# Attention heads and weight preparation in a new order: slots of broadcasts, weight loads, clearing and conversion steps

## The chip, the cores and the metric

The kernel runs on one core of a Trainium2 chip. The metric is device time in microseconds (us); a number without a unit is us. Five engines work side by side, each through its own queue in order: TensorE (PE; PEld is its weight load), VectorE (DVE), ScalarE (ACT), GpSimd (POOL) and SyncE (SP), which here only issues DMA transfers. ScalarE issues a few transfers too.

## What is computed

Attention with rotary embedding over 4 batches of 8 heads, 576 positions of 64 numbers, and then a feed-forward layer with softplus over the 2304 tokens of 512 numbers:

```python
q_rot, k_rot = (rotate(q), rotate(k))
scores = scale * np.matmul(q_rot, k_rot.transpose(0, 1, 3, 2))
attn = np.exp(scores - np.max(scores, axis=-1, keepdims=True))
attn = attn / (np.sum(attn, axis=-1, keepdims=True) + 1e-09)
x = np.matmul(attn, v)          # then heads side by side: (2304, 512)
h = x @ w_in                    # (512, 2048)
g = np.maximum(h, 0.0) + np.log1p(np.exp(-np.abs(h)))
return g @ w_out                # (2048, 512)
```

The weights come as 64-bit floats (the kernel sees int64 words); everything else is float32. A float32 operand of a matmul is split into a rounded part and a rest (names ending in h and l, or two planes of one tile), and products of the parts are summed.

## The kernel before, in words

**Slots.** Attention is written as one loop over slots `s`, five slots to a head (`h, c = divmod(s, 5)`; `c` is the slot's place in the head, and so is the last digit of `s` modulo 5). 32 heads make 160 slots. In one slot three pipelined stages work on different heads: `p1(s)` computes a block of scores of 128 rows and `tensor_reduce` its row maxima on VectorE; nine slots later (`LAG`, `n2 = s - 9`) `p2(n2)` computes the transposed scores with the maxima already subtracted, `exps` takes two exponentials on ScalarE and `low` the rest on VectorE; three slots after that (`n3 = s - 12`) `pv_mm` multiplies with V. `pv_mm` of a head's last block is followed by `evac`, a copy of the sum from PSUM by ScalarE, in slot 1 of a head.

**Shift rows.** The maxima of a head enter `p2` as two extra rows (64 and 65 of plane 1) of its tile `qs`. They take this way: GpSimd splits them (`shift1`, slot 0), TensorE transposes them and ScalarE copies them to `shr` (`shift2`, slot 1), and a transfer that ScalarE issues puts them into `qs` (`shift3`, L487, after the exponentials of slot 1). The first `p2` of that head (slot 4) needs them. There are four `qs` tiles (`NST`), so once `p2` is through with a head, the two rows are cleared for the `p1` of the head four later: L636 and L637, a ScalarE copy from a tile `zero`, which GpSimd zeroes at the start (L594).

**SyncE's order.** `chain` puts the transfers that SyncE issues one behind the other as the program writes them: for each pair of heads two raw tiles of q and k (590 KB each), per head the stacking of q and k from the rotated tiles (`stack_q`, `stack_k`), V, the store of the result (`store`), and in given slots

- a half of a weight chunk: `load_p(f, n)` in the slots of `LOADS`, 262 KB each, f the block of weights, n the half (two halves make a chunk, four a block); each chunk takes a buffer, for f = 1 of the two `wr`, else of the three `wraw`, which turn round;
- a broadcast of reciprocals of row sums: `load_r` (L186), 147 KB, 16 in all, the eight heads of batch 0 and then of batch 1, from slot `XL` on, every fifth slot. The reciprocals of a batch are made by `recip` (L569 an addition, L570 the reciprocal, both on VectorE), in slots 62, 102 and 142 for batches 0, 1 and 2.

**Conversions.** For the first three blocks the weights are converted during attention: `PLAN` has a tuple of nine slots for each of the six chunks. `conv_w` is resumed in each: a ScalarE step (L138) in the first slot and one (L151) in the second, four pieces of bit operations on VectorE (L142, L146) in the third to sixth, which are the last to read the raw tile, an addition on GpSimd (L162), a ScalarE copy (L165) in the eighth and a subtraction on GpSimd (L167). So per chunk three ScalarE steps, in the first, second and eighth slot of its tuple.

**Afterwards.** From slot 146 (`XS`) on GpSimd multiplies and splits the attention results (`split_xb`); after slot 169 the feed-forward stage begins (`emit_h`, `emit_o`), which prepares the rest of the weights beside its matmuls.

`pin` keeps an instruction in program order on its engine. GpSimd rotates q and k (`rope_steps`, one step a slot, L325 and L322), VectorE places the first pair at the start (`place_pair0`).

Of the kernel before, what the change touches and what calls it, by code (L numbers as in the profile page):

```python
# [19 lines left out]
S = 576  # L20
# [3 lines left out]
NB = 4  # L24
NH = 8
# [5 lines left out]
FC = 3  # L31
SEG = 4
XS = 146
XL = 73
WP = 160
LAG = 9
PVD = 3
NST = 4
# [3 lines left out]
PB = 5  # L42
CW = 512
AHEAD = 2
PLAN = ((78, 80, 81, 84, 86, 89, 90, 93, 95), (88, 90, 91, 94, 96, 99, 100, 103, 105),
        (98, 100, 104, 106, 109, 111, 115, 118, 120), (108, 110, 114, 116, 119, 121, 125, 128, 130),
        (120, 123, 124, 126, 129, 131, 135, 138, 140), (130, 133, 134, 136, 139, 144, 145, 148, 150))
LOADS = {43: (0, 0), 48: (0, 1), 53: (0, 2), 58: (0, 3), 63: (1, 0), 68: (1, 1), 73: (1, 2), 78: (1, 3), 83: (2, 0),
         88: (2, 1), 93: (2, 2), 98: (2, 3), 103: (3, 0), 108: (3, 1), 138: (3, 2), 143: (3, 3), 148: (4, 0), 153: (4, 1)}
SPLITS = {146: 2, 148: 0, 153: 0}  # L50
LEAD = 3
ROPES = {1: ((1, 2),), 2: ((1, 4),), 3: ((1, 1),), 5: ((1, 2),), 9: ((2, 1),), 10: ((2, 1),), 11: ((2, 1),),
# [7 lines left out]
def rope_attention_softplus_moe(  # L60
# [8 lines left out]
    nc = tc.nc  # L69
# [19 lines left out]
    pin = tc.keep_in_program_order  # L89
# [191 lines left out]
    def attention(es, es_r, es_s, tail):  # L281
# [11 lines left out]
        zero = at1.tile([128, S], F32, name="zero")  # L293
# [23 lines left out]
        def rnd(out, in_, e):  # L317
            if e == "A":
                pin(nc.scalar.copy(out=out, in_=in_))
            else:  # L320
                e = nc.vector if e == "V" else nc.gpsimd
                pin(e.tensor_scalar(out=out, in0=in_, scalar1=1.0, scalar2=0.0, op0=ALU.mult, op1=ALU.add))  # L322
# [268 lines left out]
            nc.gpsimd.memset(ks[i][64:128, 1, :].bitcast(F32), 0.0)  # L591
            nc.gpsimd.memset(ks[i][64:66, 1, :].bitcast(F32), 1.0)
        nc.gpsimd.memset(sh0.bitcast(F32), 0.0)
        nc.gpsimd.memset(zero[64:66], 0.0)  # L594
        for i in range(2):
            nc.gpsimd.memset(vs[i][:, :, 1, :].bitcast(F32), 1.0)
        place = place_pair0()
# [6 lines left out]
        for s in range(NSLOT + LAG + PVD):  # L604
            n2, n3 = s - LAG, s - LAG - PVD
            h, c = divmod(s, 5)
            r = s + 4
            if r % 10 == 0 or s == 0:
                p = r // 10 + 1
                for _ in rope:  # L610
                    pass
                rope = rope_steps(p) if 2 < p < NP else iter(())
            has2, has3 = 0 <= n2 < NSLOT, 0 <= n3 < NSLOT
            if has3 and (c != 0 or s > NSLOT):
                pv_mm(n3)
                if n3 % 5 == 4:
                    evac(n3 // 5)
                has3 = False
            if n2 < NSLOT:
                tile2(n2)  # L620
            if has2:
                p2(n2)
            shr = shift2(h - 1, n2) if s > 6 and c == 1 and s <= NSLOT + 1 else None
            if has2:
                exps(n2)
            if shr is not None:
                shift3(h - 1, shr)
            if has3:
                pv_mm(n3)
            if s < NSLOT:  # L630
                p1(s)
                if s == LAG - 2:
                    shift_first()
            if has2:
                low(n2)
            if n2 > 0 and n2 % 5 == 0 and n2 // 5 - 1 + NST < NB * NH:  # L636
                rnd(qs[(n2 // 5 - 1) % NST][64:66, 1, :S], zero[64:66], "A")  # L637
            if s >= 5 and c == 0 and s <= NSLOT:
                shift1(h - 1)
            if s == 15:  # L640
                next(sv)
            if s < NSLOT:
                if s < 2:
                    next(place)
                for p, z in ROPES.get(s, ()):
                    for _ in range(z):
                        next(pairs[p], None)
                if s == 2:
                    next(place)
                for g, i, j, a in STACKS.get(s, ()):  # L650
                    if i:
                        stack_k(g, chain, (j,))
                    else:
                        stack_q(g, chain, j, a)
                if s != 16:
                    next(rope, None)
                if s in (20, 22):
                    next(rope, None)
                g = (s + 6) // 5
                if s % 10 == 4 and 14 < s and g < NB * NH:  # L660
                    stack_q(g, chain)
                    stack_k(g, chain, (0,))
                if s % 10 == 5:
                    for _ in rope:
                        pass
                    if 15 < s and g < NB * NH:
                        stack_k(g, chain, (1,))
                if s % 10 in (2, 7) and 2 < s // 10 + 2 < NP:
                    load_pair(s // 10 + 2, (s % 10 // 7,))
                if s % 10 == 9 and s > 10 and g < NB * NH:  # L670
                    stack_q(g, chain)
                    stack_k(g, chain)
                if c == 0:
                    load_v(h)
            if c == 2 and 0 < h <= NB * NH:
                sv = split_v(h - 1)
                next(sv)
            if c == 4 and s != 14:
                next(sv, None)
            if done and c == 2:  # L680
                store(*done.pop(), chain)
            if n3 % (5 * NH) == 5 and n3 > 5:
                load_sums(n3 // (5 * NH) - 1, chain)
            if n3 % (5 * NH) == 10 and n3 > 10:
                recip(n3 // (5 * NH) - 1)
            tail(s)
        return recip

# [20 lines left out]
    with ExitStack() as es:  # L709
# [5 lines left out]
        def tail(s):  # L715
            if s == NSLOT - 9:
                es_r.close()
            i, j = divmod(s - XL, 5)
            if 0 <= i < 2 * NH and j == 0:
                load_r(*divmod(i, NH))  # L720
            if s in LOADS:
                load_p(*LOADS[s])
            for n, slots in enumerate(PLAN):
                if s == slots[0]:
                    k = divmod(n, 2)
                    early[n] = conv_w([k], CW, pin, 1, {0: pre.pop(k)}, nc.gpsimd, True)
                    next(early[n])
                if s in slots:
                    next(early[n], None)
            if s in (WP, WP + 5):  # L730
                next(late[s > WP])
            if s >= XS:
                for _ in range(2 if s > NSLOT else SPLITS.get(s, 1 if s % 5 else 0)):
                    next(splits, None)
            if s == NSLOT + LAG - 1:
                es_s.close()
                mp["h"] = pool(ctx, "ps_h", 2, space=PSUM)
                mp["t"] = pool(ctx, "t", 1)
                mp["g"] = pool(ctx, "g", NG)
            if NSLOT + LAG <= s < NSLOT + LAG + AHEAD:  # L740
                ahead.append(units[len(ahead)])
                emit_h(*ahead[-1])
            if s >= NSLOT + LAG and w.dtype != F32:
                convert()
# [92 lines left out]
```

## Time and profile before

| | us |
|---|---|
| median of 3 runs | 733.25 |
| the runs | 731.91 to 736.65 |
| the profiled execution | 732.48 |
| its span, first to last instruction | 730.60 |
| TensorE busy (share of the span) | 715.8 (98%) |
| VectorE | 493.6 (68%) |
| ScalarE | 413.7 (57%) |
| GpSimd | 318.6 (44%) |

A row of the profile has the start and the length of an instruction or of some of one kind (x4: four of them), what it writes and reads (out<-in), and in brackets the idle time of its engine before it with what ended that. L637 is line 637. Where a helper issues many operations, they all have its line: L319 is ScalarE's, L325 and L322 are VectorE's and GpSimd's. A "q" behind an engine's name (SPq, ACTq) is its queue of issues.

### The profile page before, as it was taken

Reading aid. Unit: us, or ns where it says so; the run is one execution under the profiler, and the core shown is the slowest. Engines: PE = TensorE matmul, PEld = TensorE weight load, DVE = VectorE, ACT = ScalarE, POOL = GpSimd, SP = SyncE. Lnnn points to the kernel's source line nnn. Section 1 sums busy time; section 2 is a strip of 40 time slices with the busy share of each in tenths; the row PEclk is TensorE's granted clock in tenths of the full one; section 3 lists DMA queues with packets and bytes.
Section 4 is the critical chain, followed back from the end, with each engine's and each line's share of the span. In section 5 each row is a group of like instructions: output and inputs, shape, how many; then the busy total and the mean of one; then the engine's idle time right before and its main releaser. Section 6 shows DMA issues by size and latency. Waiting matters only on the chain.

```text
span 730.6 us, 11796 instructions
## 1 busy us (share of the span) xinstructions
PE 715.8 (98%) x4282; PEld 665.2 (91%) x4282; DVE 493.6 (68%) x803; ACT 413.7 (57%) x767; POOL 318.6 (44%) x378
## 2 busy tenths in 40 slices
PE   7999999999999999999999999999999999999997
PEld 6899999998899999999989999899899998998996
DVE  7777888878798888868989986453443343434433
ACT  5888888888788888775756653232222222222222
POOL 9998888878798999681000000550500000000000
PEclk9999999999999999999999999999999999999999
DMA  7689899999998878303434331260010010001001
GB/s 257 157 204 212 208 225 229 222 209 231 226 251 219 212 212 185 81 18 96 142 96 139 119 98 50 61 200 0 22 44 0 1 45 1 0 1 44 0 1 44
DMA packets 45983, 86.98 MB, mean 119 GB/s; under 512 B 6798, under 2 KB 15684, under 8 KB 45924
## 3 DMA queue, kind: packets, MB, share of 16 engines
q1 hardware_dynamic: 42672, 80.75, 43.4%
q10 hardware_dynamic: 3252, 5.47, 2.0%
q8 instruction: 34, 0.56, 0.3%
q14 instruction: 25, 0.20, 0.1%
HBM read 48.64 MB, written 7.23 MB: 76 GB/s over the span
## 4 chain that ended last, share of the span: by engine, by line
PE 83%; DMA 8%; POOL 4%; ACT 3%; DVE 1%; issue 1%; SPq 0%; POOLq 0%
PE hp L220 28%; PE oa L256 14%; PE ob L256 14%; PE pv L534 12%; PE sp L498 9%; PE sp L452 8%; DMA ks<-raw 2%; POOL raw L325 2%; DMA qs<-raw 2%; DMA qs<-shr 2%; DMA raw<-qk 1%; ACT ph L504 1%; DMA vf<-v 1%; ACT sp L505 1%; DVE mx L454 1%
## 5 line engine op out<-in xcount | busy, mean ns | idle before, releaser
L220 PE MATMUL hp<-x,wh 128*128 128x384 f32 x768 | 196.2, 336 | 0.0
L232 ACT ACTIVATE e<-e 128x384 f32<-128x384 f32 x96 | 50.4, 525 | 201.0 <-DVE e L230 193.9
L454 DVE TENSOR_REDUCE mx<-sp 128x1 f32<-128x576 f32 x160 | 120.7, 755 | 42.7 <-PE sp L452 35.8
L220 PEld LDWEIGHTS hp<-x,wh 128*128 128x128 f32 x768 | 140.7, 188 | 8.2
L220 PE MATMUL hp<-x,wl 128*128 128x384 f32 x384 | 129.3, 337 | 0.0
L504 ACT ACTIVATE ph<-sp 128x576 fp32r<-128x576 f32 x160 | 103.9, 649 | 43.2 <-PE sp L498 38.1
L452 PE MATMUL sp<-ks,qs 128*128 128x288 f32 x640 | 114.6, 301 | 3.9 <-DVE mx L454 2.8
L498 PE MATMUL sp<-qs,ks 128*128 128x288 f32 x640 | 115.6, 301 | 2.8 <-DMA qs<-shr 2.5
L534 PE MATMUL pv<-ph,vs 128*64 128x288 f32 (+1 forms) x640 | 111.4, 296 | 1.2 <-ACT xt L544 0.6
L230 DVE TENSOR_SCALAR e<-hp 128x384 int32<-128x384 int32 x96 | 53.3, 555 | 77.6 <-PE hp L220 77.6
L513 DVE TENSOR_TENSOR pl<-sp,ph 128x576 fp32r<-128x576 f32 x128 | 96.6, 755 | 10.2 <-ACT sp L505 8.2
L505 ACT ACTIVATE sp<-sp 128x576 f32<-128x576 f32 x160 | 102.8, 642 | 0.0
L452 PEld LDWEIGHTS sp<-ks,qs 128*128 128x128 f32 x640 | 92.4, 188 | 8.7 <-DVE mx L454 5.2
L498 PEld LDWEIGHTS sp<-qs,ks 128*128 128x128 f32 x640 | 92.4, 188 | 7.9 <-DMA qs<-shr 3.5
L256 PE MATMUL oa<-wh,g 128*128 128x512 f32 x288 | 97.7, 393 | 0.0
L256 PE MATMUL ob<-wh,g 128*128 128x512 f32 x288 | 97.3, 393 | 0.0
L534 PEld LDWEIGHTS pv<-ph,vs 128*64 128x64 f32 (+1 forms) x640 | 86.6, 161 | 2.9 <-ACT xt L544 2.8
L240 DVE TENSOR_TENSOR g<-m,g 128x384 fp32r<-128x384 f32 x96 | 55.5, 578 | 47.8 <-ACT g L237 47.8
L325 POOL TENSOR_TENSOR raw<-raw 128x576 f32<-128x576 f32 (+3 forms) x62 | 86.1, 1389 | 2.6
L325 POOL TENSOR_TENSOR raw<-raw,tab 128x576 f32<-128x576 f32 x60 | 84.8, 1432 | 1.7 <-DMA raw<-qk 1.3
L235 DVE SCALAR_TENSOR_TENSOR m<-hp,e 128x384 f32<-128x384 f32 x96 | 53.5, 557 | 43.5 <-ACT e L232 42.1
L237 ACT CAST g<-m 128x384 fp32r<-128x384 f32 x96 | 49.3, 513 | 49.5 <-DVE m L235 43.8
(98 smaller groups left out, 897.1 us busy)
## 6 DMA issues: line engine op xcount, KB each, us to landing
raw<-qk SPq DMA_DIRECT2D x29, 576.0 KB
wraw<-w SPq DMA_DIRECT2D x23, 512.0 KB
ks<-raw SPq DMA_DIRECT2D x30, 320.0 KB
qs<-raw SPq DMA_DIRECT2D x27, 288.0 KB
vf<-v SPq DMA_DIRECT2D x32, 160.0 KB
ks<-raw SPq DMA_DIRECT2D x30, 160.0 KB
qs<-raw SPq DMA_DIRECT2D x30, 144.0 KB
wraw<-w SPq DMA_DIRECT2D x14, 256.0 KB
```

The costliest lines, as they stand in the source:

```text
L220: pin(nc.tensor.matmul(out=hp, lhsT=a[f][:, c * 128:(c + 1) * 128], rhs=piece(j, c)[:, b, :], start=(i == 0), stop=(i == 11),))
L235: pin(nc.vector.scalar_tensor_tensor(out=m, in0=hp, scalar=0.0, in1=e, op0=ALU.max, op1=ALU.add))
L240: pin(nc.vector.tensor_tensor(out=g[:, 1, :], in0=m, in1=g[:, 0, :].bitcast(F32), op=ALU.subtract))
L256: pin(nc.tensor.matmul(out=po, lhsT=g[:, s, t * 128:(t + 1) * 128], rhs=b[f][:, 512:1024], start=(first and i == 0), stop=(last and i == 2),))
L325: pin((nc.vector if e == "V" else nc.gpsimd).tensor_tensor(out=out, in0=in0, in1=in1, op=op))
L452: pin(nc.tensor.matmul(out=sp[:, j, :HS], lhsT=q[:, i, cq], rhs=k[:, 0, ck], start=(i == 0), stop=(i == 1)))
L454: pin(nc.vector.tensor_reduce(out=mx_t[h][:, c:c + 1], in_=sp[:, :, :HS], axis=AX.XY, op=ALU.max, negate=True))
L498: pin(nc.tensor.matmul(out=sp[:, i, :HS], lhsT=k[:, j, ck], rhs=q[:, j, hs], start=(j == 0), stop=(j == 1)))
L504: pin(nc.scalar.activation(out=ph, in_=sp, func=AF.Exp, scale=D ** -0.5))
L505: pin(nc.scalar.activation(out=sp, in_=sp, func=AF.Exp, scale=D ** -0.5))
L513: pin(nc.vector.tensor_tensor(out=pl, in0=sp[:, :, :HS], in1=ph.bitcast(F32), op=ALU.subtract))
L534: pin(nc.tensor.matmul(out=pv[rows, i, :HS], lhsT=lhs, rhs=rhs[:, i, :], start=(c == 0 and j == 0), stop=(c == 4 and j == len(terms) - 1)))
```

## The change

It moves work between slots and alters nothing that is computed. `XL` goes from 73 to 100, and the broadcasts come every third slot instead of every fifth (slots 100 to 145 instead of 73 to 148). The weight halves come ten slots earlier (from 33 on), two of the last four five slots earlier. `PLAN` is rewritten: the ScalarE steps stood in slots 0 and 3 of a head and now all stand in slot 4. The clearing of the shift rows goes from slot 4 to slot 3 of a head, one slot earlier. The tile `zero` is zeroed by VectorE in slot 9 and no longer by GpSimd at the start.

```diff
-XL = 73
+XL = 100
...
-PLAN = ((78, 80, 81, 84, 86, 89, 90, 93, 95), (88, 90, 91, 94, 96, 99, 100, 103, 105),
-        (98, 100, 104, 106, 109, 111, 115, 118, 120), (108, 110, 114, 116, 119, 121, 125, 128, 130),
-        (120, 123, 124, 126, 129, 131, 135, 138, 140), (130, 133, 134, 136, 139, 144, 145, 148, 150))
-LOADS = {43: (0, 0), 48: (0, 1), 53: (0, 2), 58: (0, 3), 63: (1, 0), 68: (1, 1), 73: (1, 2), 78: (1, 3), 83: (2, 0),
-         88: (2, 1), 93: (2, 2), 98: (2, 3), 103: (3, 0), 108: (3, 1), 138: (3, 2), 143: (3, 3), 148: (4, 0), 153: (4, 1)}
+PLAN = ((59, 64, 66, 69, 71, 74, 75, 79, 80), (69, 74, 76, 79, 81, 84, 85, 94, 95), (84, 89, 91, 94, 96, 99, 100, 109, 110),
+        (99, 104, 106, 109, 111, 114, 115, 124, 125), (114, 119, 121, 124, 126, 129, 130, 139, 140),
+        (129, 134, 136, 139, 144, 146, 150, 154, 155))
+LOADS = {33: (0, 0), 38: (0, 1), 43: (0, 2), 48: (0, 3), 53: (1, 0), 58: (1, 1), 63: (1, 2), 68: (1, 3), 73: (2, 0),
+         78: (2, 1), 83: (2, 2), 88: (2, 3), 93: (3, 0), 98: (3, 1), 133: (3, 2), 138: (3, 3), 148: (4, 0), 153: (4, 1)}
...
-        nc.gpsimd.memset(zero[64:66], 0.0)
...
-            if n2 > 0 and n2 % 5 == 0 and n2 // 5 - 1 + NST < NB * NH:
-                rnd(qs[(n2 // 5 - 1) % NST][64:66, 1, :S], zero[64:66], "A")
+            if has2 and n2 % 5 == 4 and n2 // 5 + NST < NB * NH:
+                rnd(qs[n2 // 5 % NST][64:66, 1, :S], zero[64:66], "A")
...
+                if s == 9:
+                    pin(nc.vector.memset(zero[64:66], 0.0))
...
-            i, j = divmod(s - XL, 5)
+            i, j = divmod(s - XL, 3)
```

## Rows read from the trace of the kernel before

**Rows 1.** Busy time by engine in three stages, with the columns' names
```profile
core 0: us, PE busy (x) PEld busy (x) DVE busy (x) ACT busy (x) POOL busy (x), PEclk, DMA share, GB/s
...
62.22:144.73 82.51, 82.51 (x623) 81.83 (x622) 67.25 (x93) 69.23 (x127) 69.89 (x82) 1.00 0.92 217
144.73:283.71 138.98, 134.90 (x968) 128.50 (x967) 117.86 (x191) 118.52 (x216) 121.27 (x138) 1.00 0.92 222
...
323.28:730.60 407.32, 403.06 (x2028) 364.74 (x2026) 230.07 (x410) 148.39 (x281) 40.67 (x46) 1.00 0.17 54
```

**Rows 2.** The same for heads: slot 30; 45-65; 75-105; 80; 90; 110; 115; 140
```profile
62.22:71.39 9.17, 9.17 (x72) 9.10 (x71) 7.44 (x11) 7.68 (x15) 7.76 (x10) 1.00 0.83 195
89.72:135.57 45.85, 45.85 (x348) 45.46 (x346) 37.52 (x53) 38.47 (x71) 38.82 (x46) 1.00 0.99 228
144.73:215.69 70.96, 67.90 (x486) 64.26 (x485) 57.98 (x93) 59.02 (x108) 59.35 (x68) 1.00 1.00 231
153.96:164.38 10.42, 10.27 (x71) 9.25 (x70) 8.17 (x13) 8.52 (x17) 8.04 (x11) 1.00 0.85 192
173.85:184.77 10.92, 9.93 (x70) 9.32 (x70) 8.32 (x15) 8.60 (x17) 8.93 (x10) 1.00 1.00 230
...
215.69:225.58 9.89, 9.74 (x71) 9.20 (x70) 8.39 (x15) 8.26 (x16) 7.75 (x10) 1.00 0.94 238
225.58:234.90 9.32, 9.32 (x71) 9.12 (x70) 8.38 (x15) 8.33 (x16) 8.98 (x11) 1.00 0.81 208
...
273.29:283.71 10.42, 9.80 (x71) 9.19 (x70) 9.60 (x15) 8.59 (x17) 9.21 (x12) 1.00 0.91 202
```

**Rows 3.** Timeline, the head of slot 90: a conversion, the shift, TensorE's waits
```profile
175.26 0.67 ACT L151 ACTIVATE wt<-wraw 128x512 int32<-128x512 uint32 x1
...
176.51 0.51 PEld L534 LDWEIGHTS pv<-ph,vs 128*128 128x128 f32 x4 [0.36 <-ACT xt L544]
...
178.39 0.65 ACTq L487 DMA_DIRECT2D qs<-shr  x1
179.08 0.65 ACT L504 ACTIVATE ph<-sp 128x576 fp32r<-128x576 f32 x1 [1.40 <-PE sp L452]
...
182.42 0.66 PE L498 MATMUL sp<-qs,ks 128*128 128x288 f32 x3 [0.86 <-DMA qs<-shr]
```

**Rows 4.** ScalarE's groups by line, 62 to 320 us: busy, mean ns | idle before
```profile
L319 ACT CAST qs<-zero 2x576 fp32r<-2x576 f32 x25 | 16.8, 670 | 0.6
...
L138 ACT ACTIVATE wc<-wraw 128x512 f32<-128x512 f32 x4 | 2.7, 670 | 0.0
```

**Rows 5.** The chain that ended last, near 187 us, and the timeline behind it
```profile
187.08 6.51 DMA qs<-shr
...
193.64 0.67 PE L498 MATMUL sp<-qs,ks 128*128 128x288 f32 x3 [1.60 <-DMA qs<-shr]
```

**Rows 6.** Timeline: VectorE's addition of the reciprocals (L569) and GpSimd beside it
```profile
278.93 1.43 POOL L325 TENSOR_TENSOR raw<-raw 128x576 f32<-128x576 f32 x1
...
279.10 1.30 DVE L569 TENSOR_SCALAR rc<-rc 128x36 f32<-128x36 f32 x1
...
202.25 0.95 DVE L569 TENSOR_SCALAR rc<-rc 128x36 f32<-128x36 f32 x1
...
121.61 1.44 POOL L325 TENSOR_TENSOR raw<-raw 128x576 f32<-128x576 f32 x1
...
122.86 0.23 DVE L569 TENSOR_SCALAR rc<-rc 128x36 f32<-128x36 f32 x1
```

**Rows 7.** Timeline of the start: memsets, a maximum on VectorE, TensorE's shift
```profile
3.40 0.59 DVE L588 MEMSET qs<- 64x640 f32 x1 [0.17 <-issue]
5.06 0.57 POOL L594 MEMSET zero<- 2x576 f32 x1
...
24.16 0.76 DVE L454 TENSOR_REDUCE mx<-sp 128x1 f32<-128x576 f32 x1 [0.16 <-issue]
...
25.17 0.23 PE L481 MATMUL sp<-identr,shl 128*10 128x128 f32 x1 [0.31 <-POOL shl L325]
```

## The prediction

> **What bounds the kernel now.** Read first the busy times by stage [rows 1]. From 323.28 us on TensorE is busy for 403.06 of 407.32 us: the feed-forward stage, which the change doesn't touch, has nothing to give. In attention the unit is a head, five slots. From 62.22 to 144.73 us nine heads take 82.51 us, 9.17 each, with TensorE busy all the time; this is the floor. From 144.73 to 283.71 us (the heads that start in slots 75 to 140) fourteen heads take 138.98, where the floor is 14 x 9.17 = 128.4. So 10.6 us are lost there, and they are all that a reordering of attention can win. The clock is granted in full (1.00) in every stage.
>
> Then look at single heads [rows 2]. Two patterns show. The row of seven heads from 144.73 to 215.69 takes 70.96 against 64.2: 6.8 lost, with the DMA engines at a share of 1.00 and 231 GB/s. In these heads SyncE issues a weight half (262 KB) and a broadcast (147 KB) per head on top of the attention loads. From 89.72 to 135.57 it issues the weight halves alone: 228 GB/s, share 0.99, and five heads take 45.85 = 5 x 9.17. So the DMA engines carry one extra stream at no loss and not two. The second pattern lies in the heads after that, where the transfers are few: 9.89 (slot 110) and 9.32 (slot 115); the two pairs behind them, to slot 135, repeat this within 0.05. By PLAN the long ones have a ScalarE conversion step in slot 0 of the head, the short ones only in slot 3. The last row, slot 140, 10.42, has neither.
>
> **Slot-0 conversions go.** ScalarE's step (0.67 us) runs at 175.26, ahead of the evacuation of pv; TensorE's weight load for the next pv then waits 0.36 for it [rows 3]. The price is the difference of two neighbouring heads, 9.89 - 9.32 = 0.57 [rows 2]. PLAN before has such steps in slots 80, 90, 100, 110, 120, 130; PLAN after has all 18 in slots that end in 4 or 9. Gain 6 x 0.57 = 3.4 us (bounds 0 and, if head 80's whole 10.42 - 9.17 = 1.25 were its price, 7.5; I take the rows without heavy transfers).
>
> **What slot 4 then costs.** The clearing of the shift rows (0.670) goes to slot 3, the conversion (0.67) to slot 4 [rows 4]. Before, heads like slot 115's had the conversion in 3 and the clearing in 4: the same two pieces of one length in the same two places. They lose 9.32 - 9.17 = 0.15 [rows 2], which includes VectorE's bit pieces in slot 4. The clearing itself waits for nothing new: the exponentials ahead of it already waited for the matmuls that read those rows, and what is queued behind it is the next slot's exponentials. Its cover is ScalarE's idle time, 9.17 - 7.68 = 1.49 us in a free head [rows 2]. So I put 0.15 on each of the 17 heads 55 to 135; 14 heads from 75 on pay about that already, so what is new is 4 x 0.15 = +0.6. Bounds: 0, and 18 x 0.57 if a conversion in slot 4 costs what it did in slot 0 (a rival below). VectorE's 24 pieces stay in slots 1 and 4 of a head and GpSimd's twelve steps in slot 0, at the price they had. One GpSimd step more falls behind slot 146, beside the splitting of the results; the feed-forward stage that uses these begins with TensorE busy and GpSimd idle for nine tenths [rows 1], so I put it at 0.
>
> **Weight halves ten slots earlier, broadcasts from 100 on.** SyncE issues as many transfers as before. The first fourteen weight halves now stand alone in slots 33 to 98, as in the five heads at the floor [rows 2], and the sixteen broadcasts in 100 to 145, every third slot: 147 x 5/3 = 245 KB per head, again one stream of about 256 KB. No wait for data arises: the first batch's reciprocals are written in slot 62, the second's in 102, and its first broadcast is the ninth, slot 124. Nor for buffers: half (2,0,b) in 83 reuses the raw tile whose last reader is PLAN's slot 74, (3,0) in 93 that of slot 84, (3,2) in 133 that of 129, and (4,0) in 148 that of 146. Only the last is near; behind it SyncE queues the stacking of slot 149, which is due six slots (11 us) later. What is won is the pile: of the 6.8 us of these seven heads, 3 x 0.57 were counted, 7 x 0.15 stay, and about 0.5 is the reciprocal of slot 102 (below): 3.5 are left. The rows that carry it: the shift rows' transfer, issued at 187.08, holds the chain for 6.51 us, and TensorE waits 1.60 for it, in the head before 0.86 [rows 3, 5]; and ScalarE, which issues it, idles 1.40 around the issue at 178.39 [rows 3]. I take 3.2 (bounds 0 and 3.5), since conversions now stand in heads where the margin was measured without them.
>
> One rule speaks against this term. The Trainium skill, DMA: Bandwidth & Descriptors, Queues, rings and completion order, says that each DMA engine goes round-robin between the queue rows it has work for, one packet at a time; a small transfer from ScalarE's queue should then not stand behind SyncE's pile, and thinning the pile would give the sum without these 3.2 us. The 6.51 us [rows 5] don't look like that, but no row shows where in a queue the transfer stood.
>
> **A new pile.** In slots 133 and 138 a weight half now meets broadcasts in 133, 136 and 139: some 500 KB in each of two heads, more than the 409 KB that hurt. The nearest row is slot 90's, 10.92 - 9.17 - 0.57 = +1.2 [rows 2], and that came only in the fourth piled head. Bounds 0 and 2 x 1.2 = 2.4; the attention loads of the last pairs end in slot 137, so I take +0.4.
>
> **What stays.** Slot 140's head loses 1.25 [rows 2] with no conversion in slot 0: VectorE's one small addition for the reciprocals takes 1.30 us at 279.10 and ends with the GpSimd operation that began at 278.93 and took 1.43. At 202.25 it took 0.95; at 122.86 it took 0.23, and ended with the GpSimd operation of 121.61 (1.44) [rows 6]. Slot 142 and GpSimd's work around it don't move, so I leave 1.1 there (1.25 less the 0.15 of every loaded head) and, as an estimate from 0.95 - 0.23 = 0.7, 0.5 at slot 102. The Trainium skill, SBUF — State Buffer, Who interferes with whom, has the same: VectorE and GpSimd share a port pair, and the one that comes second blocks for the whole instruction. These rows agree with it.
>
> **The zero tile.** GpSimd loses a 0.57 us memset at 5.06, in an unbroken row of setup work; at 25.17 TensorE waits 0.31 for GpSimd's shift [rows 7]: -0.3 (bounds -0.6 and 0). VectorE gains a memset in slot 9; 640 columns took it 0.59, and it has idle time of 0.16 before the maximum at 24.16 [rows 7]: +0.1 (bounds 0 and 0.6). Without that cover it would delay the maximum and the next scores by the whole 0.59.
>
> **Sum.** -3.4 + 0.6 - 3.2 + 0.4 - 0.3 + 0.1 = -5.8 us. The profiled execution took 732.48 (span 730.60 and 1.88 around it), so it would come to 726.7; the median of the runs, 733.25, lies 0.8 higher, and the forecast for the median is 733.25 - 5.8 = **727.4 us**, 0.8% less.
>
> **The rivals.**
> *The pile was not the cause.* The shift transfer stays late whatever SyncE has queued. For it: in two of the seven heads ScalarE itself was late. Against it: five heads at 0.99 without loss. The 3.2 go: 733.25 - 2.6 = 730.6. The round-robin rule of DMA: Bandwidth & Descriptors in the Trainium skill would have it so.
> *The reciprocal's stall goes too.* GpSimd has fewer conversion steps between slots 86 and 135, so its operation can start at another moment than VectorE's. Against it: GpSimd's conversion steps of slots 100 and 140 stay where they were. With 1.6 more, and no new pile, 733.25 - 7.8 = 725.4.
> *Slower: ScalarE becomes the bound.* With a clearing in slot 3 and a conversion in slot 4, 1.34 us in a row, the evacuation and the issue of the shift transfer come late in every head, as in slot 80's (10.42). For it: ScalarE is busy 8.52 of 10.42 there. Against it: slot 115's head, with the same two pieces, is busy 8.33 of 9.32 and lost 0.15 [rows 2]. With x lost in each of 18 heads, 1.6 for the reciprocals and 0.4 for the new pile, the stage loses 18x + 2.0 against 10.6 now: it decides at x = 0.48. At slot 80's 1.25 it is 24.5, 13.9 more: 747.
> That the moves do nothing is no case of its own: the slot-0 steps are gone from the program whatever the transfers do.
>
> **How the numbers follow.** About 1% (7.3 us) is what a measurement of this kernel can tell from no change. My forecast has 0.59, with its own range 724.6 to 729.8 (down: the start 0.4, the new pile 0.4, the pile 0.3, slot 4 0.6, and 0.5 each if the conversions of slots 80 and 100 cost as much as slot 80's head allows; up: the new pile 2.0 and the memset in slot 9, 0.5); 0.18 of it lies below 725.9. The pile not the cause: 0.14. The reciprocal's stall gone: 0.14, below 725.9. ScalarE the bound: 0.13, of which 0.08 for x over 0.89, over 1% slower, and 0.05 for less. Faster by over 1%: 0.32; within 1%: 0.60; slower: 0.08. The range runs from 723.5 (the third case, 725.4, with the lower bounds of the start, the pile and slot 4, 1.3 together, and 0.6 for the spread of the runs) to 732.2 (the second with the new pile at 2.0); outside are ScalarE as the bound and the tails.
>
> **What would show it.** Right: heads 80 to 130 at about 9.3, no wait of TensorE for the shift transfer between 150 and 200 us, DMA share near 1.0 from slot 33 to 145, the 1.30 us addition still there. Wrong: waits of the pv weight loads for the evacuation in most heads (ScalarE), waits for the shift transfer around slots 134 to 145 (the new pile), or the same 0.9 and 1.6 us waits with the broadcasts gone.

## The result, and the profile after

The changed kernel takes 727.82 us (median of 6 runs, 725.56 to 729.3) against 733.84 for the kernel before on the same chip (6 runs, 731.91 to 736.65). The ratio is 0.9915 with a 95% interval of 0.989 to 0.9941, so 0.85% or some 6.2 us less (the medians alone differ by 6.0). The forecast was 727.4, with 0.60 on "within 1%". The total is right; some of its terms are not, and the cause that the largest of them was put down to is wrong.

The profiled execution has a span of 723.70 us, 6.90 less than before. First its stages, the same three as in [rows 1], in the same columns:

```profile
core 0: us, PE busy (x) PEld busy (x) DVE busy (x) ACT busy (x) POOL busy (x), PEclk, DMA share, GB/s
61.66:144.98 83.32, 83.09 (x623) 82.00 (x622) 68.73 (x99) 71.27 (x130) 69.92 (x82) 1.00 0.93 220
144.98:277.15 132.17, 130.90 (x968) 127.79 (x967) 116.09 (x183) 116.10 (x212) 121.18 (x138) 1.00 0.92 229
316.77:723.70 406.93, 403.06 (x2028) 364.74 (x2026) 230.72 (x410) 148.45 (x281) 40.43 (x46) 1.00 0.17 54
```

Beside [rows 1] the reader finds where the 6.90 went. The start is 0.56 shorter (slot 30 begins at 61.66, before at 62.22). The nine heads from slot 30 on take 83.32, 0.81 more. The fourteen heads of slots 75 to 140 take 132.17, 6.81 less than the 138.98 of before. The rest of attention changes by 0.05. The feed-forward stage, which is the same program, is 0.39 shorter. The clock is granted in full throughout. The same view by heads, as in [rows 2]: slots 55; 75 to 100; 80; 90; 100; 105 to 135; 110; 140.

```profile
107.48:117.09 9.61, 9.38 (x71) 9.10 (x70) 7.34 (x11) 7.68 (x15) 7.69 (x9) 1.00 1.08 229
144.98:201.87 56.89, 56.26 (x417) 54.79 (x415) 50.50 (x81) 50.52 (x93) 52.91 (x61) 1.00 0.94 234
154.28:163.59 9.31, 9.31 (x71) 9.13 (x70) 8.35 (x15) 8.28 (x16) 8.98 (x11) 1.00 0.86 226
172.91:182.10 9.19, 9.19 (x71) 9.11 (x70) 7.89 (x13) 8.24 (x16) 7.76 (x10) 1.00 0.78 192
191.43:201.87 10.44, 9.81 (x72) 9.18 (x70) 9.61 (x15) 9.12 (x18) 9.24 (x12) 1.00 0.95 251
201.87:266.74 64.87, 64.87 (x486) 63.84 (x485) 56.02 (x89) 57.16 (x105) 59.06 (x67) 1.00 0.90 227
211.06:220.40 9.34, 9.34 (x72) 9.15 (x71) 8.38 (x15) 8.30 (x16) 9.01 (x11) 1.00 0.86 224
266.74:277.15 10.41, 9.77 (x71) 9.15 (x70) 9.58 (x15) 8.42 (x17) 9.21 (x12) 1.00 0.91 213
```

Heads 80 and 90 fell from 10.42 and 10.92 to 9.31 and 9.19, head 110 from 9.89 to 9.34. The seven heads from slot 105 to 135, among them those of the feared new pile (slots 133 to 139), take 64.87, 0.7 over seven times the 9.17 of the floor. Two long heads are left, slot 100 with 10.44 and slot 140 with 10.41. Head 55 is new among the longer ones (9.17 before). It and head 70 (9.42, before 9.16) carry most of the 0.81 that the nine heads from slot 30 on lost. What TensorE's weight loads wait for between 150 and 200 us, where [rows 3, 5] had shown TensorE waiting 0.86 and 1.60 for the shift transfer (columns: what waited, for whom, us in total, times, longest):

```profile
PEld sp L452 <- DVE mx L454: 0.9, 1, 0.9
```

The shift transfer is gone from that list. The one wait that is left comes from the addition of the reciprocals in slot 102, as the timeline shows; it answers to [rows 6]:

```profile
197.08 1.44 POOL L325 TENSOR_TENSOR raw<-raw 128x576 f32<-128x576 f32 x1
197.24 1.31 DVE L569 TENSOR_SCALAR rc<-rc 128x36 f32<-128x36 f32 x1
...
198.89 0.69 DVE L454 TENSOR_REDUCE mx<-sp 128x1 f32<-128x576 f32 x1
199.63 0.56 PEld L452 LDWEIGHTS sp<-ks,qs 128*128 128x128 f32 x4 [0.86 <-DVE mx L454]
```

The addition begins 0.16 after a GpSimd operation and ends with it. Before, in this slot, it took 0.95; now 1.31, as in slot 142. Behind it stand the reciprocal and then the maximum, and TensorE's next scores wait for the PSUM bank that the maximum reads. Last the start, which answers to [rows 7]:

```profile
23.87 0.54 DVE L645 MEMSET zero<- 2x576 f32 x1 [0.17 <-issue]
...
24.44 0.76 DVE L454 TENSOR_REDUCE mx<-sp 128x1 f32<-128x576 f32 x1
...
24.55 0.23 PE L481 MATMUL sp<-identr,shl 128*10 128x128 f32 x1
```

VectorE's memset (0.54) lies right ahead of the maximum. TensorE's shift matmul, at 25.17 before, comes at 24.55.

### The profile page after: what moved, and what is told of

Read it like the earlier page. It is cut to its first block, busy times and chain, and to the rows that moved or that the text cites. A ratio compares the mean times of both kernels' runs of the same rounds, so it can differ in the third digit from the quotient of the medians.

```text
span 723.7 us, 11796 instructions
## 1 busy us (share of the span) xinstructions
PE 712.5 (98%) x4282; PEld 665.2 (92%) x4282; DVE 495.0 (68%) x804; ACT 413.9 (57%) x767; POOL 317.9 (44%) x377
## 4 chain that ended last, share of the span: by engine, by line
PE 93%; DMA 3%; DVE 2%; ACT 1%; issue 0%; SPq 0%; DVEq 0%
PE hp L220 28%; PE pv L534 15%; PE oa L256 14%; PE ob L256 14%; PE sp L498 11%; PE sp L452 11%; DMA qs<-shr 1%; DVE mx L454 1%; DMA raw<-qk 1%; DMA ks<-raw 0%; DVE rc L569 0%; ACT xt L544 0%; PE sp L481 0%; ACT ph L504 0%; DVE ks L325 0%
## 5 line engine op out<-in xcount | busy, mean ns | idle before, releaser
L452 PE MATMUL sp<-ks,qs 128*128 128x288 f32 x640 | 114.0, 300 | 4.2 <-DVE mx L454 3.7
L498 PE MATMUL sp<-qs,ks 128*128 128x288 f32 x640 | 114.5, 300 | 0.6 <-DMA qs<-shr 0.4
L452 PEld LDWEIGHTS sp<-ks,qs 128*128 128x128 f32 x640 | 92.4, 188 | 8.5 <-DVE mx L454 5.8
L498 PEld LDWEIGHTS sp<-qs,ks 128*128 128x128 f32 x640 | 92.2, 188 | 4.8 <-DVE ph L516 1.0
```

What stands on the lines that cost most here:

```text
L452: pin(nc.tensor.matmul(out=sp[:, j, :HS], lhsT=q[:, i, cq], rhs=k[:, 0, ck], start=(i == 0), stop=(i == 1)))
L498: pin(nc.tensor.matmul(out=sp[:, i, :HS], lhsT=k[:, j, ck], rhs=q[:, j, hs], start=(j == 0), stop=(j == 1)))
```

## The experiments

The change has three parts that matter: the broadcasts, the conversion steps and the clearing. The first six runs do or undo them, one or two at a time. One view tells the mechanisms apart: the waits of TensorE's weight loads between 20 and 300 us, in which "qs<-shr" is the shift transfer and "xt L544" the evacuation. In the changed kernel they are:

```profile
PEld sp L498 <- DMA qs<-shr: 0.8, 2, 0.5
PEld pv L534 <- ACT xt L544: 0.5, 1, 0.5
```

and in the kernel before:

```profile
PEld sp L498 <- DMA qs<-shr: 3.5, 4, 1.8
PEld pv L534 <- ACT xt L544: 2.8, 7, 0.8
```

One wait for the evacuation, of 0.5 to 0.8 near slot 16, stands in every kernel. Before had six more, of 2.0 together, in the six heads with a conversion in slot 0. All ratios below are to the kernel before on the same chip, whose medians were 733.6 to 734.3. The us named beside a ratio are worked out from it and can lie about a us off the difference of two medians; the intervals are given behind the ratios, and 0.001 is 0.73 us.

**The broadcasts alone.** The kernel before with

```diff
-XL = 73
+XL = 100
-            i, j = divmod(s - XL, 5)
+            i, j = divmod(s - XL, 3)
```

> The kernel before with the broadcasts in slots 100 to 145 alone. Two weight halves (slots 103, 108) and two late ones still meet broadcasts. Theory: heads 85, 95 and 105 come near 9.3, heads 80 to 130 with a ScalarE step in slot 0 stay at 9.9, no wait for the shift transfer between slots 75 and 100; about 3 us under before, 730.8. Rival (the pile was not the cause): waits of 0.9 and 1.6 us for the shift transfer stay in heads 90 and 95, within 0.7 us of before.

Measured: 730.75 us, ratio 0.9958 (0.994 to 0.9976), some 3.1 us less.

```profile
PEld sp L498 <- DMA qs<-shr: 2.6, 5, 1.4
PEld pv L534 <- ACT xt L544: 2.3, 5, 0.8
```

The heads with a conversion in slot 0 stay long, with five waits for the evacuation, and the waits for the shift transfer shrink from 3.5 to 2.6. In the heads of slots 75 to 100, where the pile was, they went from 3.1 in three waits to 0.4 in one; the longest, 1.4, is new and stands in head 50.

**The broadcasts back.** The changed kernel with the same two lines as before.

> The changed kernel with the broadcasts back in slots 73 to 148, every fifth; all else as changed. Weight halves and broadcasts meet from slot 73 to 98, six heads. Theory: the pile's price returns without any ScalarE step in slot 0, some 2.6 us over the changed kernel (730.4), in heads 80 to 100, with waits for the shift transfer. Rival (pile not the cause): the changed kernel's time, 727.8.

Measured: 731.68, ratio 0.9966 (0.9948 to 0.9984), which is 3.7 us more than the changed kernel's 0.9915.

```profile
PEld sp L498 <- DMA qs<-shr: 5.3, 6, 1.3
PEld pv L534 <- ACT xt L544: 0.5, 1, 0.5
```

Here the evacuation waits are gone and those for the shift transfer are back. The two runs give the pile's price from both sides: 3.1 with it taken from before (1.8 to 4.4 by the interval), 3.7 with it put back (some 2 either way).

Part of these waits lies ahead of the transfer. In most heads ScalarE issues it 0.04 us behind the end of the copy to `shr`. In before it came 2.00 and 1.78 behind in heads 80 and 90, in the run with the broadcasts back 1.49 and 1.37, in the run with the broadcasts alone 0.14 and 0.37, though ScalarE's steps in that run are those of before. In head 95 it is the landing: the last packet came 5.1 behind the issue in before, 3.2 in the run with the broadcasts alone. So the second stream goes with late issues as well as with a late landing. What such an issue waited for, no row shows.

**Conversions and clearing alone.** The kernel before with the new `PLAN` and the clearing in slot 3:

```diff
+PLAN = ((59, 64, 66, 69, 71, 74, 75, 79, 80), ...
...
+            if has2 and n2 % 5 == 4 and n2 // 5 + NST < NB * NH:
+                rnd(qs[n2 // 5 % NST][64:66, 1, :S], zero[64:66], "A")
```

> The kernel before with the new PLAN and the clearing in slot 3 alone; weight halves and broadcasts stay where they were (two streams from slot 73 to 108). Theory (the terms add up: a ScalarE step in slot 0 costs 0.57 us, the pile of transfers some 3.2): heads 110, 120 and 130 fall from 9.9 to 9.3, the waits of TensorE for the shift transfer between slots 90 and 100 stay; about 3 us under before, 730.8. Rival (the pile was not the cause, ScalarE alone made the shift transfers late): the waits go too, and nearly the whole gain is there, 6 us under before, 727.8.

Measured: 732.65, ratio 0.9982 (0.9963 to 1.0), some 1.3 us less where about 3 were expected.

```profile
PEld sp L498 <- DMA qs<-shr: 7.1, 8, 2.2
PEld pv L534 <- ACT xt L544: 0.5, 1, 0.5
```

The six evacuation waits go, and the heads of slots 110 to 135 fall to between 9.2 and 9.55. But the waits for the shift transfer double, from 3.5 to 7.1, with the transfers as they were. Read so, TensorE meets again at the next late transfer much of what it wins elsewhere: while the pile stands, taking other work off the path mostly moves the wait. This run and the one with the broadcasts back differ only in the ten slots of the weight halves and in the memset; their ratios, 0.9982 and 0.9966, lie 1.2 us apart with intervals that overlap, so those two parts have no price that can be told from nothing.

**The conversions back in slot 0.** The changed kernel with all eighteen ScalarE steps in slot 0 of a head, the clearing left in slot 3:

```diff
-PLAN = ((59, 64, 66, 69, 71, 74, 75, 79, 80), ...
+PLAN = ((60, 65, 66, 69, 71, 74, 75, 80, 81), ...
```

> The changed kernel with all 18 ScalarE conversion steps one slot later, in slot 0 of a head (and GpSimd's subtraction one slot later); clearing in slot 3, transfers as changed. Theory: 0.45 to 0.57 us for each of 17 heads, 8 to 10 us over the changed kernel (736 to 738), with waits of the pv weight loads for the evacuation in every head. Rival (the place of the step costs nothing once the transfers are spread): the changed kernel's time, 727.8.

Measured: 728.19, ratio 0.9919 (0.9892 to 0.9946): no cost that can be told from the changed kernel's 0.9915, where 8 to 10 us were expected. The step by which a conversion in slot 0 costs 0.57 by itself falls.

**The clearing back in slot 4.** The changed kernel with the two lines of the clearing as they were before, the conversions left in slot 4.

> The changed kernel with the clearing back in slot 4, ahead of the conversion step there. Theory (ScalarE has 1.5 us free per head, but the evacuation in slot 1 comes two exponential pairs later): 1.34 us in one slot run past it and push slot 0 and the evacuation, by less than a step in slot 0 does: 0.2 to 0.5 in each of 17 heads, 3 to 8 us over the changed kernel (731 to 736). Rival (the free time of slot 0 swallows it): the changed kernel's time, 727.8, and the clearing's move was worth nothing.

Measured: 736.14, ratio 1.0023 (1.0003 to 1.0044), 7.9 us more than the changed kernel.

```profile
PEld sp L498 <- DMA qs<-shr: 7.4, 7, 1.7
PEld pv L534 <- ACT xt L544: 5.0, 16, 0.8
```

Sixteen evacuation waits now, fifteen of them new. The slots behind them lengthen by 0.25 to 0.47 each, 4.7 us in the heads of slots 60 to 140, and the waits for the shift transfer go from 0.8 to 7.4. (The profiled execution, 738.75, is the slowest of the ten and lies 13.2 above the changed kernel's, so these waits don't add up to the 7.9.) ScalarE's timelines show why the evacuation is late. In them "the scores of slot 0" are those of `p1` (L452), with which a head begins in the tables above. First the run with the conversions in slot 0, in the head whose scores of slot 0 begin at 231.02:

```profile
228.67 0.67 ACT L319 CAST qs<-zero 2x576 fp32r<-2x576 f32 x1
...
230.48 0.65 ACT L504 ACTIVATE ph<-sp 128x576 fp32r<-128x576 f32 x1
...
231.69 0.67 ACT L151 ACTIVATE wt<-wraw 128x512 int32<-128x512 uint32 x1
232.27 0.64 ACT L544 COPY xt<-pv 65x576 f32<-65x576 f32 x1
```

Then the kernel before, in its head of slot 120, whose scores of slot 0 begin at 234.90, with the weight load that waits:

```profile
234.41 0.67 ACT L319 CAST qs<-zero 2x576 fp32r<-2x576 f32 x1
235.11 0.65 ACT L504 ACTIVATE ph<-sp 128x576 fp32r<-128x576 f32 x1
...
236.33 0.68 ACT L138 ACTIVATE wc<-wraw 128x512 f32<-128x512 f32 x1
236.91 0.61 ACT L544 COPY xt<-pv 65x576 f32<-65x576 f32 x1
...
237.58 0.51 PEld L534 LDWEIGHTS pv<-ph,vs 128*128 128x128 f32 x4 [0.34 <-ACT xt L544]
```

And the run with the clearing back in slot 4, scores of slot 0 from 240.99:

```profile
240.48 0.67 ACT L319 CAST qs<-zero 2x576 fp32r<-2x576 f32 x1
241.17 0.68 ACT L151 ACTIVATE wt<-wraw 128x512 int32<-128x512 uint32 x1
241.74 0.64 ACT L504 ACTIVATE ph<-sp 128x576 fp32r<-128x576 f32 x1
...
242.84 0.64 ACT L544 COPY xt<-pv 65x576 f32<-65x576 f32 x1
```

The conversion stands right ahead of the evacuation in the first and in the second of them. What differs is the clearing. In the first it is done before the exponentials of slot 4; those of slot 0 begin at 230.48, 0.54 ahead of the scores of slot 0, and the evacuation begins 1.25 behind those scores. In the second the clearing stands between the two pairs of exponentials, those of slot 0 begin at 235.11, 0.21 late, and the evacuation begins 2.01 behind; its end is what the weight load waits for. In the third both pieces stand ahead of slot 0's exponentials, and the evacuation begins 1.85 behind. In the changed kernel, with one piece in that place, it begins 1.26 to 1.28 behind in all seventeen heads from slot 60 to 140; in the kernel before 1.98 to 2.05 in the six heads with both pieces, 1.25 to 1.37 in the eleven others. So between the exponentials of slot 4 and the evacuation ScalarE has room for one piece of 0.67, in slot 4 or in slot 0, and mostly not for two (in the run with the clearing back, two of the seventeen heads with both pieces, 65 and 105, have no wait for the evacuation). That was the cost of the six long heads.

**The clearing alone.** The kernel before with the two lines of the clearing in slot 3, and nothing else.

> The kernel before with one edit: the clearing of the shift rows goes from slot 4 of a head to slot 3, all else (conversion steps, weight halves, broadcasts) stays. Theory: the 0.57 us of the heads of slots 110, 120 and 130 came from the clearing in slot 4 and the conversion in slot 0, two ScalarE pieces in a row ahead of the evacuation. Then those heads fall from 9.9 to about 9.3 with their conversions still in slot 0, and the waits for the shift transfer in the heads of slots 80 to 100 stay or grow: about 731 to 732.5 us, ratio 0.996 to 0.998. Rival: the conversion's slot was the cause, as the prediction had it; the heads stay at 9.9 and the time at about 734.

Measured: 735.45, ratio 1.0025 (1.0 to 1.0049), no gain. Neither the theory's numbers nor the rival's reason hold.

```profile
PEld sp L498 <- DMA qs<-shr: 5.2, 5, 2.3
PEld sp L498 <- DVE wc L146: 3.6, 7, 0.6
...
PEld pv L534 <- ACT xt L544: 0.5, 1, 0.5
```

The evacuation waits do go, as the theory said. But the `PLAN` of before has its other conversions in slot 3, and there the clearing now makes a new pair. The timeline from slot 108 to 111:

```profile
215.34 0.67 ACT L319 CAST qs<-zero 2x576 fp32r<-2x576 f32 x1
216.02 0.70 ACT L138 ACTIVATE wc<-wr 128x512 f32<-128x512 f32 x1
...
217.83 0.76 DVE L513 TENSOR_TENSOR pl<-sp,ph 128x576 fp32r<-128x576 f32 x1 [0.50 <-ACT sp L505]
...
218.95 0.29 DVE L146 SCALAR_TENSOR_TENSOR wc<-wr,sp 128x128 int32<-128x128 int32 x1
219.29 0.56 PEld L498 LDWEIGHTS sp<-qs,ks 128*128 128x128 f32 x4 [0.59 <-DVE wc L146]
```

Both pieces stand in a row, the exponentials come late, VectorE waits 0.50 for them, and its bit piece, which borrows a PSUM bank of the scores (`sp`), gives the bank back late; the scores of slot 1 wait 0.59 for it. In the sum of these waits the evacuations fell by 2.3 (2.8 to 0.5), the bank took 3.6 and the shift transfer 1.7 more: the pair costs as much there as ahead of the evacuation, through another engine. The heads bear it out: 125 and 135, with no conversion in slot 0 but one in the slot 3 ahead of them, rose from 9.28 and 9.31 to 9.92 and 9.84, and 110, 120 and 130, with both, stay at 9.83, 9.81 and 9.70. This is why the clearing and the conversions had to end up apart, and why the two moves can't be priced one by one.

**VectorE's pieces.** With the ScalarE pair apart, some 0.13 us are left in slot 0 (1.77 for 1.64, from its `p1` scores to the next) of eleven heads (70 to 85, 95, 100, 110, 115, 125, 130, 140). They stand behind the heads in which a bit piece of VectorE lies in slot 4, and are missing behind those with a conversion alone there (90, 105, 120, 135); one such piece, in slot 144, has none behind it. Two runs move those pieces, to slot 3 and to slot 2:

```diff
-PLAN = ((59, 64, 66, 69, 71, 74, 75, 79, 80), ...
+PLAN = ((59, 64, 66, 68, 71, 73, 75, 79, 80), ...      # slot 3
+PLAN = ((59, 64, 66, 67, 71, 72, 75, 79, 80), ...      # slot 2
```

> The changed kernel with VectorE's bit pieces of slot 4 one slot earlier, in slot 3. Theory (the 0.13 us in slot 0 of most loaded heads is VectorE's piece in slot 4, not ScalarE's conversion there): heads of 9.32 fall to 9.2, about 1.4 us under the changed kernel (726.4). Rival (the conversion in slot 4 costs the 0.13): the changed kernel's time, 727.8.

> The changed kernel with VectorE's bit pieces that stand in slot 4 of a head (they cost 0.13 us in the slot behind it, eleven times) put in slot 2 of the same head. The PSUM bank that such a piece uses is taken next by the scores of slot 4, which run behind the pv matmuls of that slot, so TensorE has work until the bank is free. Theory: the 0.13 go in eleven heads, 1.4 us: about 726.4. Rival: the piece meets the reduction of VectorE or a GpSimd operation in slot 2 or holds its bank as in the run with the pieces in slot 3: 729 or more.

Measured: 735.27, ratio 1.0026 (1.0007 to 1.0044), and 729.62, ratio 0.9936 (0.9911 to 0.996). Both expectations failed. In slot 3:

```profile
218.20 0.29 DVE L146 SCALAR_TENSOR_TENSOR wc<-wr,sp 128x128 int32<-128x128 int32 x1
...
218.63 0.77 PE L498 MATMUL sp<-qs,ks 128*128 128x288 f32 x4 [0.54 <-DVE wc L146]
```

The 0.13 went, and the transposed scores of slot 0 (L498), which take that bank, wait 0.54 instead, with nothing of TensorE's ahead of them to cover it: in slot 0 the program has these scores ahead of the pv matmuls, in the others behind them. With the piece in slot 2 VectorE comes late to its share of slot 3's block (L516), and the transposed scores of slot 0 wait for that bank:

```profile
PEld sp L498 <- DVE ph L516: 2.9, 12, 0.4
```

(0.8 in three waits in the changed kernel). The piece costs 0.13 in slot 4, about 0.3 in slot 2 and 0.7 in slot 3. Where the change left it is the cheapest of the three.

**The addition on GpSimd.** The changed kernel with L569 on GpSimd and the reciprocal six slots later:

```diff
-            pin(nc.vector.tensor_scalar(out=r, in0=r, scalar1=1e-9, scalar2=0.0, op0=ALU.add, op1=ALU.add))
+            pin(nc.gpsimd.tensor_scalar(out=r, in0=r, scalar1=1e-9, scalar2=0.0, op0=ALU.add, op1=ALU.add))
```

> The changed kernel with the addition to the sums on GpSimd instead of VectorE, in the same slots (62, 102, 142), and the reciprocal on VectorE six slots later. Theory (VectorE's addition is held by the GpSimd operation that runs beside it): heads 100 and 140 fall from 10.4 to about 9.3, 2.2 us under the changed kernel (725.6), and GpSimd's addition takes about 0.2 us with no wait for the transfer of the sums. Rival (the sums' transfer lands late): GpSimd waits for that transfer, and its lateness shows in the rotation behind it.

Measured: 726.8, ratio 0.9906 (0.9878 to 0.9934), which can't be told from the changed kernel's 0.9915.

```profile
198.53 0.34 POOL L569 TENSOR_SCALAR rc<-rc 128x36 f32<-128x36 f32 x1
```

and the waits for the shift transfer, as above:

```profile
PEld sp L498 <- DMA qs<-shr: 2.7, 5, 0.7
```

The addition takes 0.34 there and the stalls of heads 100 and 140 are gone (9.38 and 9.32). But the waits for the shift transfer go from 0.8 to 2.7: in the profiled execution most of what was won is met again at late transfers. With the pieces in slot 2 as well:

> The same with the reciprocals' addition on GpSimd as well. Theory: both gains add, 1.4 for the pieces and 2.5 for the two stalls of the addition, and late shift transfers take about 1.3 back, as in the run with the addition alone: about 725.2, ratio 0.988. Rival: the shift transfer's waits take all of it: about 727 to 728.

Measured: 727.9, ratio 0.9907 (0.988 to 0.9934). No version beats the changed kernel by more than these runs can tell.

**The memset.** The changed kernel with `zero` zeroed by GpSimd at the start, as before.

> The changed kernel with the zero tile zeroed by GpSimd at the start again. Read from the start of slot 30's scores, which came at 62.22 us before and at 61.66 in the changed kernel. Theory: GpSimd's row of setup work carries the difference, slot 30 at 62.0 to 62.3. Rival (the clearing's move or a transfer made it): slot 30 at 61.7.

Measured: 726.67 in one run; slot 30 begins at 61.98 (61.66 in the changed kernel, 62.22 before). That would make the memset worth about 0.3. But slot 30 begins anywhere from 61.36 to 61.92 in the eight kernels with VectorE's memset and the clearing in slot 3, which differ only behind slot 30; with GpSimd's memset and the clearing in slot 3 it begins at 61.89, 61.98 and 62.39. The sign looks right, the size stays open.

**The place of the weight halves.** The changed kernel with sixteen halves three slots later:

```diff
-LOADS = {33: (0, 0), 38: (0, 1), 43: (0, 2), ...
+LOADS = {36: (0, 0), 41: (0, 1), 46: (0, 2), ...
```

> The changed kernel with the sixteen weight halves of slots 33 to 98, 133 and 138 three slots later, in slot 1 of a head and not in slot 3; broadcasts, conversions and clearing stay. In the order of SyncE they then stand behind the load of V and ahead of the store and the next stacking, close before ScalarE issues the transfer of the shift rows. Theory: that transfer lands behind what SyncE has just put out, so a half (262 KB, at the 228 GB/s of these stages 1.15 us) lands ahead of it in at least every second head, where its margin is 0.6 to 3 us: waits for it in several of the heads of slots 35 to 95, 729 to 732 us. Rival: the small transfer does not queue behind SyncE's; the waits stay about as they are, 727 to 728 us.

Measured: 726.37, ratio 0.9918 (0.9883 to 0.9954), on the rival's side.

```profile
PEld sp L498 <- DMA qs<-shr: 2.7, 7, 0.8
```

There are more waits (seven for two), all short, in heads 25, 50 to 60, 100, 130 and 140, and the time doesn't move. The issue of the transfer came 1.37, 1.81 and 1.27 us behind the copy in heads 40, 50 and 140, so a late issue doesn't need a second stream. So where in a head the single stream is issued matters little; whether a second stream lies on top of it (the two runs with the broadcasts) matters.

## Why the prediction was right, and where it was not

**The pile: right.** Predicted 3.2, measured 3.1 and 3.7 by the two runs that move the broadcasts alone. In the heads of slots 75 to 100 of the changed kernel the DMA share fell from 0.99 to 0.94, and the waits for the shift transfer between 150 and 200 us are gone. The first rival falls: the transfer does not stay late whatever SyncE has queued. The Trainium skill (DMA: Bandwidth & Descriptors, Queues, rings and completion order) has each DMA engine take turns between the queue rows that it has work for, a packet at a time. From that rule the prediction had made its case against this term, and the term came all the same; but no row shows in which order an engine took the packets, and a half moved close ahead of the transfer cost nothing, so the rule itself is neither borne out nor refuted. What holds the transfer, or its issue, is not shown, only that a second stream does. One sign did not come: a DMA share near 1.0 from slot 33 to 145 was expected, and it was 0.93, 0.94 and 0.90 in the heads of slots 30 to 70, 75 to 100 and 105 to 135.

**Slot-0 conversions: the step failed.** The prediction read "by PLAN the long ones have a ScalarE conversion step in slot 0" and charged 0.57 to that slot. The difference of the two heads was read rightly, its cause not: the run with all conversions in slot 0 costs nothing. The short heads of before had one piece between the exponentials of slot 4 and the evacuation, the clearing; the long ones had two, the clearing and the conversion. The prediction saw the clearing in both and so left it out of the difference, and put its move at nothing. The term came out (heads 110, 120 and 130 went from 9.90, 9.91 and 9.90 to 9.34, 9.19 and 9.32), because one of the two pieces left that place: the clearing, and not the conversion, which the change only moved within it. That the sum held here is luck: the prediction counted the right heads for a wrong reason.

**The slower rival was misread for the same reason.** It asked whether a clearing in slot 3 and a conversion in slot 4 cost x in each head; they cost 0. But its picture, "1.34 us in a row", came true in two runs: with clearing and conversion both in slot 4 (7.9 us), and both in slot 3 of the old `PLAN`. The change stands one slot away from the first of them.

**Slot 4: the size about right, the owner only in part.** Predicted 0.15 in each loaded head, VectorE's pieces included; measured 0.13 in those behind a bit piece of VectorE and about 0 in those behind the conversion alone. The sum for slots 55 to 70 was +0.6; the stage of [rows 1] that ends there grew by 0.81, of which 0.44 is one wait for the shift transfer in head 55 that the prediction did not have, and 0.26 lies in head 70:

```profile
114.74 0.43 PEld L498 LDWEIGHTS sp<-qs,ks 128*128 128x128 f32 x3 [0.46 <-DMA qs<-shr]
```

**The new pile: at its lower bound.** Predicted +0.4 with bounds 0 and 2.4. No wait for the shift transfer stands in the heads of slots 130 to 140; 135 takes 9.20.

**The reciprocals: half right.** Slot 142's 1.25 stayed, as said. In slot 102 the estimate was 0.5 (from 0.95 - 0.23); the addition took 1.31 and the head loses 1.27 over the floor. The estimate carried a duration over, though what sets it is where in GpSimd's operation the addition begins, and the heads ahead of it had moved. The second rival, that the stall goes too, falls. The Trainium skill (SBUF — State Buffer, Who interferes with whom) says of a VectorE operation in a two-port mode that, against GpSimd, the one that issues second blocks until the other is through. The rows agree once more, 1.31 beside GpSimd's 1.44, ending together; in which mode VectorE ran, no row shows.

**The start: -0.56 for -0.2.** The sign is right and the size within the bounds' reach; how much of it the memset made is open.

**Sum.** By steps the prediction had -3.4 + 0.6 - 3.2 + 0.4 - 0.3 + 0.1. The fourteen heads from slot 75 on were to become 6.2 shorter (-3.4 - 3.2 + 0.4) and became 6.81 shorter; the rest of the 6.90 is the start (-0.56), the stage ahead (+0.81) and -0.34 behind slot 145. The runs split the total so: the broadcasts alone 3.1; all the rest, once they have moved, 3.2 (0.9958 to 0.9915), where the prediction's terms for it come to 2.6; but with the broadcasts where they were the same rest is worth 2.5 (0.9966), each with some 2 us either way. The median's 6.2 and the forecast's 5.8 differ by less than the interval of the measurement (0.989 to 0.9941 is 4.3 to 8.1 us).

**What stays open.** Waits for the shift transfer come and go at heads 25, 55 and 85 in runs that differ elsewhere: the run with the clearing in slot 4 has 1.2 to 1.7 in heads 25, 45 and 55, ahead of the first conversion, the changed kernel 0.4 and 0.5 in two of them, and before has 0.3 once there. How that run's 7.9 us divide between its evacuations and such waits is therefore not settled. The ten slots of the weight halves were not undone alone. Nor was it tried to take the transfer off ScalarE's queue, which would tell a late issue from a late landing.

## What to carry to other kernels

Two neighbours in a profile that differ in a step's place may differ in its distance to another step: before a price is put on a slot, write down, in both, the engine's whole row of work up to the instruction that is waited for, with the pieces that both have. Move the suspected step alone and its partner alone; here the clearing moved alone gave nothing, the conversions moved without it gave a loss, and with both moved the waits went. And where a small transfer has little margin under a loaded DMA, work taken off elsewhere is partly met again at that transfer, so the gains of separate edits don't add.

## What the runs showed of the hardware that was not expected

- A 5 KB transfer issued by ScalarE had its last packet 1.4 to 5.1 us behind its issue in the kernel before, in the heads of slots 30 to 140, and 1.4 to 4.1 in the changed one, with DMA shares of 0.8 to 1.1 in these heads. TensorE needs it some 4.7 us behind the end of the copy ahead of it. The issue itself stood 0.04 us behind that copy in most heads and up to 2.0 in single heads of before. The place of a 262 KB load within the head did not move the time, a second stream of 147 KB per head did.
- ScalarE took in one extra piece of 0.67 us between the exponentials of slot 4 and the evacuation with no loss, and a second one cost 0.3 to 0.6 in nearly every head that had it. No idle time shows in its row from the exponentials of slot 4 on in either case; what shows is where the evacuation begins, 1.26 or 1.8 to 2.05 us behind the scores of slot 0.
- VectorE's addition of 36 columns took 0.23 to 1.31 us in attention, by where in a GpSimd operation it began ([rows 6] and above), and 0.34 on GpSimd itself.
